# Two small reorderings in an attention and SwiGLU kernel: key sums scaled group by group, and the value copies of the first two batches dealt out anew between VectorE and ScalarE

## The chip, the cores and the metric

The kernel runs on one core of a Trainium2 chip. A core has TensorE (matrix products into eight PSUM banks), VectorE and ScalarE (which read PSUM and write SBUF), GpSimd ([...]it also issues most loads here) and SyncE (issues stores and transposing loads). The engines run side by side and wait for one another by semaphores; each works through its own instructions in order. The metric is the time of one execution on the device in microseconds; lower is better. Before the change it was 236.28 us, the median of four runs (235.95 to 236.55).

## The reference

For 8 batches of 8 heads, with 576 positions, head size 64 and 32 memory slots, attention goes over slots that are softmax-weighted sums of keys and values; its output, 4608 rows of 512, goes through a SwiGLU block with inner width 1536.

```python
a = exp(phi - max(phi)); a = a / (sum(a over slots) + 1e-9)
k_m = einsum('bhsm,bhsd->bhmd', a, k)
v_m = einsum('bhsm,bhsd->bhmd', a, v)
attn = softmax(q @ k_m.T / sqrt(64))
x = (attn @ v_m) as rows of 512
out = (silu(x @ w_gate) * (x @ w_val)) @ w_out
```

## The kernel before, in words

The kernel never forms `attn @ v_m`. It multiplies the memory values `v_m` of a batch into the gate and value weights first (a projection round, `u_round`, L454), which gives small matrices `U` for each batch, chunk of 512 inner columns and group of four heads; the attention weights `A` are then multiplied straight into `U`. Groups are called g = 0 and 1 throughout, and each has its own PSUM bank in a round.

The order of the work is written out by hand: Python calls emit instructions one after another, each engine's queue holds its instructions in that order, and there is no automatic reordering. PSUM banks come from a first-in, first-out list `free` of eight names: `bank` (L75) takes the first, `done` (L81) puts one back at the end. A matmul into a bank waits until the last instruction that read the bank's earlier tile has finished.

Loads of the first stage are issued by GpSimd in one sequence (L880 to L908): keys, queries and values of the first batches, then the weights, those of the first chunk in two halves (L897 to L899), those of the second and third chunks (L900 to L902), and the output weights.

**Batches 0 and 1** are prepared together. After their attention weights are there, the rounds of chunk 0 are split into halves of 256 columns and into gate (`which` 0) and value (`which` 1) parts, `u_half` (L829). Each such round makes 8 matmuls `p_u` into two banks, one per group, and copies each bank into `U` with the denominator as a scale (L488 on ScalarE for the letter "a", L492 on VectorE for "v"; the letters of `evac` go to the banks in order, group 0 first). The sequence is L945 to L957: gate round of batch 0 ("av"), of batch 1 ("vv"), four gates of batch 0 (`gv_gate`, L518: two matmuls `p_g`, a silu on ScalarE at L526), then the value rounds of batch 0 and 1, two gates of batch 1, then three value products (`flush_mul(3)`: two matmuls `p_v` each, and a product `t_h` on VectorE at L532), then the second half of chunk 0 for both batches, and so on. A `p_v` of batch 0 needs the value part of `U` of both groups of batch 0.

**Batches 2 to 7** are each taken through in one stage. Their memory keys and values come from `kv_sum` (L222): 72 matmuls add into two banks `p_kv0` and `p_kv1`, one per group, the keys in columns 0 to 63 and the values in columns 64 to 127; the denominators go into a corner of `p_kv0`. `kv_norm` (L268) then makes four scaled copies on VectorE (`scaled_copy`, L265): keys of group 0 (written twice side by side, 128 elements), keys of group 1, values of group 0 (64 elements), values of group 1. After it `run_sums` (L295) gives both banks back, and `kv_T` transposes the result: on TensorE up to batch 3, by a transposing transfer on SyncE after that. For batches 3 and 5 the denominators are made ahead of the sums and the copies precede the rest of the round; for batches 4, 6 and 7 another round stands between (`behind`). Beside all this run the gates and products of the batch before, whose slots take the banks as they come free, and the output products (L720).

Of the kernel before, what the change touches and what calls it, by code (L numbers as in the profile page):

```python
# [14 lines left out]
def kernel(  # L15
# [28 lines left out]
    NG = 2  # L44
# [30 lines left out]
    def bank(shape, dtype, name):  # L75
        tag = free.pop(0)
        t = ps.tile(shape, dtype, tag=tag, name=name)
        held[id(t)] = tag, t
        return t

    def done(*tiles):  # L81

        for t in tiles:
            free.append(held.pop(id(t))[0])
# [137 lines left out]
    def kv_sum(b, p, parts):  # L222


        w0, w1 = parts[0], parts[-1] + 1
        n = (w1 - w0) * D
        for j in range(JK):
            for i in range(NP):
                for g in range(NG):
                    nc.tensor.matmul(  # L230
                        p[g][32 * i:32 * i + 32, 0:n],
                        lhsT=phi_of(b, g, j, i),
                        rhs=kvs[b][64 * g:64 * g + 64, w0:w1, i, j * D:(j + 1) * D],
                        start=(j == 0),
                        stop=(j == JK - 1),
                        tile_position=(64 * g, 32 * i),
                    )

    def kv_denominators(b, p):

        if b in masked:
            for g in range(NG):
                for j in range(JK):
                    nc.tensor.matmul(
                        p[:, g:g + 1],
                        lhsT=masked[b][:, j, g].rearrange("p i m -> p (i m)"),
                        rhs=ones1,
                        start=(j == 0),
                        stop=(j == JK - 1),
                    )  # L250
            return
        if b in esums:
            hl = esums.pop(b)
            terms = [hl[:, t] for t in range(2)]
        else:
            terms = [ephis[b][:, j].rearrange("p i m -> p (i m)") for j in range(JK)]
        for n, x in enumerate(terms):
            nc.tensor.matmul(p, lhsT=x, rhs=ones2, start=(n == 0), stop=(n == len(terms) - 1))

    def kv_reciprocal(b, p):  # L260
        r = att.tile([128, NG], FP32, tag="rS", name="t_rS")
        nc.vector.reciprocal(out=r, in_=p)
        rSs[b] = r

    def scaled_copy(out, p, r):  # L265
        nc.vector.tensor_scalar(out=out, in0=p, scalar1=r, scalar2=None, op0=ALU.mult)  # L266

    def kv_norm(b, p):  # L268

        t = att.tile([128, 3, 128], BF16, tag="bkv", name="t_bkv")  # L270
        for g in range(NG):
            x = p[g][:, 0:D].rearrange("p (a d) -> p a d", a=1).to_broadcast([128, 2, D])
            scaled_copy(t[:, g].rearrange("p (a d) -> p a d", a=2), x, rSs[b][:, g:g + 1])
        for g in range(NG):
            scaled_copy(t[:, 2, D * g:D * g + D], p[g][:, D:2 * D], rSs[b][:, g:g + 1])
        bkvs[b] = t

    def kv_T(b):


        kTs[b] = att.tile([128, 3, 128], BF16, tag="kT", name="t_kT")
        t = bkvs.pop(b)
        if b > 3:
            nc.sync.dma_start_transpose(out=kTs[b], in_=t.rearrange("p n x -> p (n x)"))
            return
        p = bank([128, 3, 128], BF16, "p_T")
        for n in (2, 0, 1):
            nc.tensor.transpose(p[:, n], t[:, n], ident)
        nc.vector.tensor_copy(out=kTs[b], in_=p)
        done(p)  # L290

    def kv_items(b, beside=None):


        def run_sums():  # L295
            o = 2 * D
            p = [bank([128, CH], FP32, f"p_kv{g}") for g in range(NG)]
            behind = b in esums
            if not behind:
                kv_denominators(b, p[0][:, o:o + NG])  # L300
            kv_sum(b, p, (0, 1))
            if behind:
                beside()
                kv_denominators(b, p[0][:, o:o + NG])
            kv_reciprocal(b, p[0][:, o:o + NG])
            kv_norm(b, p)
            done(*p)
            if beside and not behind:
                beside()

        return [run_sums, lambda: kv_T(b)]
# [142 lines left out]
    def u_round(b, parts, evac):  # L454


        banks = []
        for which, c, halves in parts:
            w0, w1, h0, h1 = which[0], which[-1] + 1, halves[0], halves[-1] + 1
            n = (h1 - h0) * HC  # L460
            p = [bank([128, CH], FP32, f"p_u{g}") for g in range(NG)]
            for w in which:
                o = (w - w0) * n
                for i in range(NP):
                    for g in range(NG):
                        nc.tensor.matmul(  # L466
                            p[g][32 * i:32 * i + 32, o:o + n],
                            lhsT=kTs[b][64 * g:64 * g + 64, 2, 32 * i:32 * i + 32],
                            rhs=w_part(w, c, i, g, halves),
                            start=True,  # L470
                            stop=True,
                            tile_position=(64 * g, 32 * i),
                        )
            for g in range(NG):
                if (b, c, g) not in Us:
                    u_buffer(b, c, f"U{c}")
                if len(which) == 1:
                    dst = Us[b, c, g][:, h0:h1, w0]
                else:
                    dst = Us[b, c, g][:, h0]  # L480
                src = p[g][:, 0:(w1 - w0) * n].rearrange("p (a f) -> p a f", f=HC)
                banks.append((dst, src, p[g], rSs[b][:, g:g + 1] if b in scaled else None))
        for (t, p, home, r), e in zip(banks, evac):
            if e == "a":
                if r is None:
                    nc.scalar.copy(out=t, in_=p)  # L486
                else:
                    nc.scalar.activation(out=t, in_=p, func=AF.Copy, scale=r)  # L488
            elif r is None:
                nc.vector.tensor_copy(out=t, in_=p)  # L490
            else:
                nc.vector.tensor_scalar(out=t, in0=p, scalar1=r, scalar2=None, op0=ALU.mult)  # L492
            done(home)
# [24 lines left out]
    def gv_gate(b, s):  # L518

        jf, r = s // 2, s % 2  # L520
        c, o = jf // 4, jf % 4
        if o == 0 and r == 0:
            hts[b, c] = hpool.tile([128, 4, S], BF16, tag=f"h{c}", name="t_h")
        gate = gv_half(b, s, 0)
        sg = work.tile([128, HALF], BF16, tag="sg", bufs=8, name="t_sg")
        nc.scalar.activation(out=sg, in_=gate[:, 0:HALF], func=AF.Silu)  # L526
        done(gate)
        dst = hts[b, c][:, o, r * HALF:(r + 1) * HALF]

        def mul():  # L530
            val = gv_half(b, s, 1)
            nc.vector.tensor_tensor(out=dst, in0=sg, in1=val[:, 0:HALF], op=ALU.mult)  # L532
            done(val)
            if o == 3 and r == 1:
                chunk_done(b, c)

        pend.append(mul)
# [291 lines left out]
    def u_half(b, which, c, half, evac):  # L829

        return lambda: u_round(b, ((which, c, (half,)),), evac)
# [8 lines left out]
    def run(items):  # L840
        for x in items:
            x()
# [13 lines left out]
    def gv_slots(b):  # L856
        return [lambda s=s: gv_slot(b, s) for s in range(2 * NJF)]
# [90 lines left out]
    run([u_half(1, (0,), 0, 0, "vv")])  # L948
    for s in range(4):
        gv_gate(0, s)  # L950
    run([u_half(0, (1,), 0, 0, "va"), u_half(1, (1,), 0, 0, "va")])
    for s in range(2):
        gv_gate(1, s)
    flush_mul(3)
# [33 lines left out]
    for b in range(2, B):  # L988
# [59 lines left out]
        g = gv_slots(b)  # L1048
# [61 lines left out]
```

## Time and profile before

| | |
|---|---|
| median of four runs | 236.28 us (235.95 to 236.55) |
| the profiled execution | 236.13 us |
| its span, first to last instruction | 234.2 us |
| granted TensorE clock, mean | 0.995 |
| value matmuls `p_v`, 128x288 (L509) | 384 of 286 ns |
| silu of a gate (L526) | 192 of 424 ns |
| product `t_h` on VectorE (L532) | 192 of 451 ns |
| table load on ScalarE ahead of the silus (L946) | 1.28 us |
| scaled copies of the key sums (L266) | 24, of 273 to 352 ns |

Lengths of matmuls are from start to a modelled end, and they overlap: two of 128x288 that follow one another start 0.12 us apart. Instructions on VectorE and ScalarE overlap a little at their ends, too. A line of the timeline merges instructions of one kind that follow one another: its first number is the start, the second the time from there to the end of the last, `xN` their number. PE is TensorE's matmuls, PEld its weight loads, DVE VectorE, ACT ScalarE, POOL GpSimd. In a line of waits stand the engine and line that waited, who released it, the total in us, how many times, and the longest.

### The profile page before, as it was taken

How to read it: one execution, taken by the hardware profiler on the slowest of the kernel's cores; microseconds unless marked ns; L12 is line 12 of the kernel's file. 1: busy time of each engine (PE TensorE's matmuls, PEld its weight loads, DVE VectorE, ACT ScalarE, POOL GpSimd, SP SyncE). 2: the span in 40 equal slices, each digit the busy share in tenths (PEclk: the TensorE clock that was granted, in tenths of full speed). 3: DMA queues.
4: the chain of work that ended last, by engine and by line, in shares of the span. 5: the costliest groups of instructions: out<-in, count | busy, mean ns of one | idle time of the engine just before them, and what ended most of it. 6: DMA issues, size and time to landing. Idle time of an engine off the chain costs nothing.

```text
span 234.2 us, 7201 instructions
## 1 busy us (share of the span) xinstructions
PE 224.1 (96%) x2825; PEld 169.8 (73%) x2825; DVE 183.2 (78%) x421; ACT 173.7 (74%) x369; POOL 140.6 (60%) x190
## 2 busy tenths in 40 slices
PE   7987899999999999999999999999999999999992
PEld 2554466778887776878788787887788778878881
DVE  4155789999966698989797767999799879977732
ACT  2768788988447889968896658968898789677220
POOL 8422536998199059765966689464845494039390
PEclk9999999999999999999999999999999999999997
DMA  6999999999995992999099946995022702201224
GB/s 213 210 212 207 197 206 207 236 232 263 207 238 133 257 254 46 231 217 163 29 260 212 200 122 119 254 218 93 10 82 95 121 0 94 90 34 58 63 76 134
DMA packets 36610, 36.84 MB, mean 157 GB/s; under 512 B 14560, under 2 KB 30944, under 8 KB 36576
## 3 DMA queue, kind: packets, MB, share of 16 engines
q0 software_dynamic: 16272, 22.42, 51.5%
q1 hardware_dynamic: 19536, 13.18, 22.2%
q10 hardware_dynamic: 768, 0.79, 1.1%
q8 instruction: 22, 0.36, 0.6%
q14 instruction: 12, 0.10, 0.1%
HBM read 42.47 MB, written 9.44 MB: 222 GB/s over the span
## 4 chain that ended last, share of the span: by engine, by line
PE 86%; DMA 7%; ACT 2%; POOL 1%; DVE 1%; issue 1%; POOLq 0%
PE p_v L509 20%; PE p_os L720 20%; PE p_g L509 20%; PE p_oc L720 10%; DMA t_kv<-in_v_dram 7%; PE p_oa L720 5%; PE p_u L466 5%; PE p_kv L230 2%; PE p_g L390 1%; POOL t_kv L99 1%; DVE t_bkv L266 1%; PE p_mT L319 1%; PE p_warm L867 1%; ACT t_sg L526 1%; ACT L946 1%
## 5 line engine op out<-in xcount | busy, mean ns | idle before, releaser
L532 DVE TENSOR_TENSOR t_h<-t_sg,p_v 128x288 bf16<-128x288 bf16 x192 | 81.8, 451 | 17.9 <-PE p_v L509 6.9
L509 PEld LDWEIGHTS <-t_U 128*128 128x128 bf16 x768 | 73.6, 98 | 23.8 <-issue 3.8
L526 ACT ACTIVATE t_sg<-p_g 128x288 bf16<-128x288 f32 x192 | 74.0, 424 | 17.9 <-PE p_g L509 11.5
L509 PE MATMUL p_v<-t_A,t_U 128*128 128x288 bf16 x384 | 77.3, 286 | 0.4 <-ACT t_U L488 0.4
L509 PE MATMUL p_g<-t_A,t_U 128*128 128x288 bf16 x384 | 77.1, 286 | 0.6 <-ACT t_U L488 0.4
L720 PEld LDWEIGHTS <-t_S 128*128 128x128 bf16 x384 | 37.5, 98 | 4.5 <-issue 0.2
L597 POOL TENSOR_TENSOR t_S<-t_h 128x512 bf16<-128x512 bf16 x17 | 19.6, 1155 | 32.8 <-DVE t_h L532 32.7
L720 PEld LDWEIGHTS <-t_h 128*128 128x128 bf16 x288 | 27.1, 98 | 8.6 <-issue 5.0
L486 ACT CAST t_U<-p_u 128x512 bf16<-128x512 f32 x53 | 28.0, 607 | 6.6 <-PE p_u L466 6.6
L720 PE MATMUL p_os<-t_T,t_S 128*128 128x256 bf16 x192 | 23.7, 273 | 0.0
L554 POOL TENSOR_TENSOR t_S<-t_S,t_h 128x512 bf16<-128x512 bf16 x17 | 19.6, 1154 | 1.3
L554 POOL TENSOR_TENSOR t_S<-t_h,t_S 128x512 bf16<-128x512 bf16 x16 | 18.4, 1152 | 0.0
L554 POOL TENSOR_TENSOR t_S<-t_h 128x512 bf16<-128x512 bf16 x16 | 18.4, 1151 | 0.0
L466 PE MATMUL p_u<-W,t_kT 64*32 64x512 bf16 (+1 forms) x416 | 15.7, 364 | 0.3 <-DVE t_kT L333 0.3
L867 PE MATMUL p_warm<-bones 128*128 128x512 bf16 x44 | 13.3, 443 | 1.7 <-DVE bones L889 1.7
L720 PE MATMUL p_os<-t_T,t_h 128*128 128x256 bf16 x96 | 14.8, 273 | 0.0
L490 DVE CAST t_U<-p_u 128x512 bf16<-128x512 f32 x19 | 12.4, 683 | 1.9 <-PE p_u L466 1.9
L446 DVE TENSOR_TENSOR t_A<-t_E,t_lz 128x576 bf16<-128x576 bf16 x16 | 11.4, 739 | 0.7 <-ACT t_lz L422 0.7
L720 PE MATMUL p_oc<-t_T,t_S 128*128 128x256 bf16 x96 | 11.9, 273 | 0.0
L720 PE MATMUL p_oa<-WO,t_h 128*128 128x256 bf16 x96 | 11.8, 273 | 0.0
L720 PE MATMUL p_oc<-WO,t_S 128*128 128x256 bf16 x96 | 11.8, 272 | 0.1
L720 PE MATMUL p_os<-WO,t_h 128*128 128x256 bf16 x96 | 11.8, 272 | 0.0
(106 smaller groups left out, 308.5 us busy)
## 6 DMA issues: line engine op xcount, KB each, us to landing
out_dram<-t_o SPq DMA_DIRECT2D x15, 512.0 KB, 3.7
t_kv<-in_k_dram POOLq DMA_DIRECT2D x8, 576.0 KB, 10.3
t_q<-in_q_dram POOLq DMA_DIRECT2D x8, 576.0 KB, 8.7
t_kv<-in_v_dram POOLq DMA_DIRECT2D x8, 576.0 KB, 14.9
t_phi<-in_phi_dram POOLq DMA_DIRECT2D x6, 576.0 KB, 8.2
WO<-in_moe_w_out_dram POOLq DMA_DIRECT2D x3, 512.0 KB, 19.5
W<-in_moe_w_gate_dram POOLq DMA_DIRECT2D x2, 512.0 KB, 16.3
W<-in_moe_w_val_dram POOLq DMA_DIRECT2D x2, 512.0 KB, 16.2
```

What stands on the lines that cost most here:

```text
L230: nc.tensor.matmul(p[g][32 * i:32 * i + 32, 0:n], lhsT=phi_of(b, g, j, i), rhs=kvs[b][64 * g:64 * g + 64, w0:w1, i, j * D:(j + 1) * D], st ...
L446: nc.vector.tensor_tensor(out=a, in0=es.pop((b, g)), in1=lzs.pop((b, g)), op=ALU.mult)
L466: nc.tensor.matmul(p[g][32 * i:32 * i + 32, o:o + n], lhsT=kTs[b][64 * g:64 * g + 64, 2, 32 * i:32 * i + 32], rhs=w_part(w, c, i, g, halve ...
L486: nc.scalar.copy(out=t, in_=p)
L490: nc.vector.tensor_copy(out=t, in_=p)
L509: nc.tensor.matmul(p[:, 0:HALF], lhsT=Us[b, c, g][:, o // 2, which, 128 * (o % 2):128 * (o % 2 + 1)], rhs=atts[b, g][:, r], start=(g == 0) ...
L526: nc.scalar.activation(out=sg, in_=gate[:, 0:HALF], func=AF.Silu)
L532: nc.vector.tensor_tensor(out=dst, in0=sg, in1=val[:, 0:HALF], op=ALU.mult)
L554: eng.tensor_tensor(out=out, in0=x, in1=y, op=ALU.subtract)
L597: eng.tensor_tensor(out=t[:, 0], in0=A21, in1=A22, op=ALU.add)
L720: nc.tensor.matmul(mine[home][:, u], lhsT=lhs(c, m, u), rhs=rhs(c, m), start=fresh and u == 0, stop=(k == 5), skip_group_check=u == 1 or n ...
L867: nc.tensor.matmul(p[:, 0:128 * a], lhsT=bones, rhs=x.to_broadcast([128, a, 128]) if a > 1 else bones, start=True, stop=True,)
```

## The change

Two edits. In `kv_norm` the two copies of a group now follow one another (keys and values of group 0, then keys and values of group 1), and each group's bank is given back right after its copies, in place of both after the four. In the first stage the letters of the value rounds change: batch 0's copies both go to VectorE and batch 1's both to ScalarE, where each batch had one on either.

```diff
@@ kv_norm
         for g in range(NG):
             x = p[g][:, 0:D].rearrange("p (a d) -> p a d", a=1).to_broadcast([128, 2, D])
             scaled_copy(t[:, g].rearrange("p (a d) -> p a d", a=2), x, rSs[b][:, g:g + 1])
-        for g in range(NG):
             scaled_copy(t[:, 2, D * g:D * g + D], p[g][:, D:2 * D], rSs[b][:, g:g + 1])
+            done(p[g])
         bkvs[b] = t
@@ run_sums
             kv_reciprocal(b, p[0][:, o:o + NG])
             kv_norm(b, p)
-            done(*p)
             if beside and not behind:
                 beside()
@@ first stage
     for s in range(4):
         gv_gate(0, s)
-    run([u_half(0, (1,), 0, 0, "va"), u_half(1, (1,), 0, 0, "va")])
+    run([u_half(0, (1,), 0, 0, "vv"), u_half(1, (1,), 0, 0, "aa")])
     for s in range(2):
         gv_gate(1, s)
     flush_mul(3)
```

The banks come free in the same order as before, so every tile keeps its bank. On VectorE the second and third of the four scaled copies change places, in each of the six batches, and one copy of the first stage is that of another tile; on ScalarE one copy is that of another tile. TensorE's, GpSimd's and SyncE's instructions keep their order; on TensorE three instructions of the first stage wait for something else.

## The prediction

> **What bounds the kernel now.** I read the page's busy rows first, then the waits of TensorE and its weight loads, then the timeline of the two places that the change touches.
>
> ```profile
> PE 224.1 (96%) x2825; PEld 169.8 (73%) x2825; DVE 183.2 (78%) x421; ACT 173.7 (74%) x369; POOL 140.6 (60%) x190
> ```
>
> TensorE's instructions fill the span, and the chain that ended last is 86% TensorE. After the last warm-up stall, at 21.1 us, that chain leaves TensorE for only a few tenths at a time, so a hold of TensorE moves the end, and a microsecond of VectorE or ScalarE that holds nobody moves nothing. The waits of the matmuls (first fence) and of the weight loads (second) say which holds there are:
>
> ```profile
> PE p_v L509 <- ACT t_U L488: 0.4, 1, 0.4
> ```
>
> ```profile
> PEld L509 <- ACT t_U L488: 1.3, 2, 0.7
> PEld L509 <- DVE t_bkv L266: 0.8, 2, 0.4
> ```
>
> One hold of the value matmuls `p_v` by ScalarE's copy of a `t_U`, and two of 0.4 us by `t_bkv`. (The other hold in the 1.3 is at 26.5 us, in front of the first gate; the change leaves it.) The first of them, on the timeline of 23.5 to 36 us; columns are start, length from first start to last end, engine, line, operation, and in brackets the idle time before:
>
> ```profile
> 27.10 1.76 DVE L492 TENSOR_SCALAR t_U<-p_u,t_rS 128x256 bf16<-128x256 f32 x4
> 27.78 1.32 ACT L526 ACTIVATE t_sg<-p_g 128x288 bf16<-128x288 f32 x4
> 28.85 0.28 PE L509 MATMUL p_v<-t_A,t_U 128*128 128x288 bf16 x1
> 28.96 0.86 ACT L488 ACTIVATE t_U<-p_u,t_rS 128x256 bf16<-128x256 f32 x2
> 29.51 0.79 PE L509 MATMUL p_v<-t_A,t_U 128*128 128x288 bf16 x5 [0.38 <-ACT t_U L488]
> 29.67 0.75 ACT L526 ACTIVATE t_sg<-p_g 128x288 bf16<-128x288 f32 x2
> 29.92 1.18 DVE L532 TENSOR_TENSOR t_h<-t_sg,p_v 128x288 bf16<-128x288 bf16 x3 [1.06 <-ACT t_U L488]
> 30.23 0.63 PE L466 MATMUL p_u<-W,t_kT 64*32 64x256 bf16 x32
> 30.74 1.26 ACT L488 ACTIVATE t_U<-p_u,t_rS 128x512 bf16<-128x512 f32 x2 [0.32 <-PE p_u L466]
> 31.02 1.40 DVE L492 TENSOR_SCALAR t_U<-p_u,t_rS 128x512 bf16<-128x512 f32 x2
> ```
>
> VectorE's four copies are the gate pair of batch 1, then group 0 of the value round of batch 0, then group 0 of that of batch 1; starts 27.10, 27.49, 27.98, 28.38, end 28.86. ScalarE, late because of the table load at 26.49 (1.28 us), first does four silus and only then group 1 of batch 0 and group 1 of batch 1. So the first `p_v` gets its first matmul at 28.85 and its second, which needs group 1 of batch 0, at 29.51. Meanwhile VectorE has nothing to do for 1.06 us: it had copied batch 1's half, which nobody wants yet. The second place, on the timeline of 80.5 to 87 us (132 us looks the same):
>
> ```profile
> 82.12 0.99 DVE L266 TENSOR_SCALAR t_bkv<-p_kv,t_rS 128x128 bf16<-128x128 f32 x4
> 82.98 0.36 PEld L509 LDWEIGHTS <-t_U 128*128 128x128 bf16 x4 [0.37 <-DVE t_bkv L266]
> 83.24 0.41 PE L509 MATMUL p_v<-t_A,t_U 128*128 128x288 bf16 x2
> ```
>
> VectorE's four scaled copies start at 82.12, 82.39, 82.65 and 82.84. The gate at 82.98 takes the bank of `p_kv0`, given back by the third of them; the value matmuls at 83.24 take that of `p_kv1`, given back by the fourth at 82.12 + 0.99 = 83.11.
>
> **Part 1, the value rounds.** No instruction is added or removed: one 128x256 copy changes from ScalarE to VectorE (rows: 484 ns median there, 499 ns the shortest on ScalarE) and one comes back. No bank is handed out in another order, and TensorE's program differs only in what three instructions wait for.
> - VectorE now does group 1 of batch 0 in the slot of batch 1's group 0: 28.38 to 28.86. The bank rows show 0.05 to 0.08 us from an end to TensorE's restart (29.43 to 29.51 here, 82.93 to 82.98 there), so the second matmul may start at about 28.93, while unheld it would start at 28.97. The 0.54 us excess in 28.85 to 29.51 (0.66 less the 0.12 of one matmul) is gone.
> - What is late next: the second `p_v` takes the bank of the fourth silu, which ends at 29.10, so 29.17; TensorE is ready at 29.10. Behind this new wait stand the third `p_v` and the projection round; VectorE's products wait for them. Three `p_v` then end at 29.17 + 2 x 0.245 = 29.66 instead of 30.12, and the next projection round starts at about 29.77 instead of 30.23: gain 0.46.
> - Its banks: VectorE's (28.86), ScalarE's two copies, which end at about 29.43 and 29.82 as before, and that of the first silu of batch 1 (29.67 + 0.41 = 30.08, usable 30.15). So the second half of the round starts at 30.15 instead of 30.51: gain 0.36. The next `p_v` takes the bank of the second silu, 30.42 + 0.07 = 30.49 instead of 30.79: gain 0.30. ScalarE has become the limit, and it can win no more than its own idle 0.32 in front of 30.74.
> - Then a little comes back. After the casts at 31.02 to 32.42 TensorE's pairs, 0.245 us apart elsewhere, are 0.28, 0.29 and 0.36 apart three times up to 33.20, 0.20 us over, for banks that VectorE returns late. VectorE starts its three products at about 29.36 instead of 29.92 and its casts some 0.55 us earlier, against 0.30 for TensorE, so most of these holds go. Gain at the end of the stage between 0.30 and 0.50; I take 0.45, near the upper end, since the largest hold (33.20) waits on a product that VectorE then does half a microsecond sooner.
> - Of batch 1, both groups are now ScalarE's: group 0 is ready at 29.43 instead of 28.86. Its first reader is a product of TensorE at about 30.7, so 1.2 us of other work covers that. As a bank it is wanted at 29.77, with 0.27 to spare; without the cover it would cost what it is late.
> - Behind: the next round needs the value weights' second chunk. Its load was issued at 17.67 and took 16.9, so landed at 34.6; TensorE reads it at 35.01 + 0.28 = 35.29 now and at about 34.84 then. At the loads before, TensorE started 0.05 to 0.07 us after the landing, so there is 0.15 us left: this caps the gain at about 0.6.
>
> **Part 2, the key sums.** The same 24 copies, in another order. A 128-wide copy is followed by the next after 0.27 us, a 64-wide one after 0.19. So the copies start at 82.12, 82.39, 82.58 and 82.84, `p_kv0` comes back with the second (about 82.67 instead of 82.93) and `p_kv1` with the fourth, as before at 83.11. The gate starts at about 82.72, 0.26 us sooner, and then the value matmuls wait for 83.16: won are 83.24 - 83.16 = 0.08, less some 0.015 for starting anew. The Trainium skill's page "PSUM — Partial Sum Buffer" (section "PSUM bank collisions raise a hardware error") bears on this: readers and writers are kept apart by bank, not by address. If only the first returned bank counted, the two places would give 2 x 0.26 = 0.52; with the second bank held to the fourth copy, as rule and row have it, 2 x 0.065 = 0.13. Below nothing it could go if a second stop of TensorE exposed a whole weight load (98 ns in the row): 2 x (0.08 - 0.10) = -0.04. I take 0.13, because the restart at 82.98 reached its next pair after 0.26 us against 0.245 in the unheld row. In the other four batches the four copies move past nothing: at 60.9 the next user is the transposes, which read all four results, and at 106, 159 and 183 us the banks are taken again only later, with no wait in the rows. VectorE's products behind the four copies start as before. No DMA is moved, and the queues of SP and GpSimd are unchanged.
>
> A rule against any gain is in "Perfetto Trace Analysis", section "Identifying the Most-Contended Engine": work on the engine of highest occupancy. Here that is TensorE, of whose work nothing is removed; by that rule alone the sum is 0 and the time 236.13. The rows show the holds by name (0.38 + 0.37 + 0.40), on the engine that sets the end; so I count these, of which the above gives back half.
>
> **Sum.** The profiled execution took 236.13 us (span 234.2 and 1.9 around it). 0.45 + 0.13 = 0.58 off: 235.55. That execution lies 0.15 below the median of 236.28; for the median, 235.70. After 34 us nothing that I find takes it back: TensorE has no wait over 0.4 us, and the last sums on GpSimd start behind VectorE's sums, which start behind TensorE.
>
> **Rivals.**
> - The gain is lost on the way (no change). ScalarE is busy without a break from 26.0 to 30.42; if the holds up to 33.20 are ScalarE's and not VectorE's, and the second stops of part 2 cost a weight load each, 0.30 - 0.04 = 0.26 remains: 236.02; a landing at 34.8 would take 0.1 more. For it: every bank that TensorE wants from 29.1 to 30.5 is ScalarE's. Against: VectorE, not ScalarE, is the later one at 33.20.
> - Slower: the weight load sets the pace at 35 us. TensorE arrives there sooner, and if the second value chunk lands at L, the round starts at L + 0.07 instead of 35.29. From L = 35.22 the gain of part 1 is gone, and with part 2's 0.13 it is slower by over 0.47 us from L = 35.8; L = 36 gives 236.28 + 0.78 - 0.13 = 236.93. For it: the weight loads took 15.5 to 19.8 us, a spread of 4.3. Against: nothing in the change touches their issue, all before 25 us, and the runs before lie within 0.6 us.
> - More: both banks of the key sums count in full, 0.50 + 0.52: 235.26. Against it stands the fourth copy at 83.11.
>
> **Numbers.** About 0.2%, or 0.47 us, is what a measurement of this kernel can tell from no change. Forecast 0.58 off (taken between 0.34 and 0.65): chance 0.65, of which some 0.08 falls short of 0.47. No change 0.19, slower 0.11, more 0.05. So faster 0.62, within 0.27, slower 0.11. The range from 235.2 to 236.4 takes in the first, second and fourth case and leaves out the slower one and some scatter.
>
> **What would show it.** Right: the wait of `p_v` for ScalarE's `t_U` is gone, the three `p_v` stand together by 29.7, the projection round near 29.8 and the next near 34.55; at 82 us the gate starts near 82.7 instead of 82.98, and the value matmuls follow after a second short stop, under 0.1 us sooner than now. Wrong: a wait for a weight load at 34.6, a new hold by ScalarE at 30 to 33, or the next rounds (35.0, 39.6) standing where they stand now.

## The result, and the profile after

The changed kernel takes 235.81 us (median of 28 runs, 235.47 to 236.50), against 236.35 for the kernel before in 46 runs: a ratio of 0.9979, 95% interval 0.9973 to 0.9984, or 0.50 us faster (0.38 to 0.64). The forecast was 0.58 us less than 236.28, or 235.70. The profiled execution took 235.82 us with a span of 233.9.

TensorE is still what fills the span, and the hold of `p_v` by ScalarE's `t_U` is gone: the waits of the matmuls have no line of `p_v` any more (first fence: the page; second: waits of the weight loads):

```profile
PE 223.4 (95%) x2825; PEld 169.6 (73%) x2825; DVE 183.3 (78%) x421; ACT 173.7 (74%) x369; POOL 140.6 (60%) x190
```

```profile
PEld L508 <- ACT t_U L487: 0.7, 1, 0.7
PEld L508 <- DVE t_bkv L266: 0.7, 2, 0.3
```

Of ScalarE's `t_U` only the wait ahead of the first gate is left. The two stops by `t_bkv` are still there, now 0.3 instead of 0.4 at the most. (All line numbers after L307 are one lower than before.) The value rounds, on the timeline of 26.9 to 36 us:

```profile
27.40 1.76 DVE L491 TENSOR_SCALAR t_U<-p_u,t_rS 128x256 bf16<-128x256 f32 x4
29.15 0.95 PE L508 MATMUL p_v<-t_A,t_U 128*128 128x288 bf16 x6
29.26 0.86 ACT L487 ACTIVATE t_U<-p_u,t_rS 128x256 bf16<-128x256 f32 x2
29.67 1.18 DVE L531 TENSOR_TENSOR t_h<-t_sg,p_v 128x288 bf16<-128x288 bf16 x3 [0.51 <-PE p_v L508]
30.04 0.85 PE L465 MATMUL p_u<-W,t_kT 64*32 64x256 bf16 x32
30.48 0.14 PEld L465 LDWEIGHTS <-t_kT 64*32 64x32 bf16 x14 [0.21 <-issue]
30.55 1.32 ACT L487 ACTIVATE t_U<-p_u,t_rS 128x512 bf16<-128x512 f32 x2
32.79 0.41 PE L508 MATMUL p_g<-t_A,t_U 128*128 128x288 bf16 x2
33.03 0.41 PE L508 MATMUL p_v<-t_A,t_U 128*128 128x288 bf16 x2
34.84 0.63 PE L465 MATMUL p_u<-W,t_kT 64*32 64x512 bf16 x16
```

The same stretch before, the lines that are compared with these (timeline of 23.5 to 36 us):

```profile
26.53 1.15 PE L509 MATMUL p_g<-t_A,t_U 128*128 128x288 bf16 x8 [0.36 <-ACT t_U L488]
32.84 0.41 PE L509 MATMUL p_g<-t_A,t_U 128*128 128x288 bf16 x2
33.20 0.41 PE L509 MATMUL p_v<-t_A,t_U 128*128 128x288 bf16 x2
35.01 0.62 PE L466 MATMUL p_u<-W,t_kT 64*32 64x512 bf16 x16
```

The three `p_v` stand together in one row of six matmuls. The projection round behind them begins at 30.04 and stops once, at 30.48, at its second half. After it ScalarE goes on without a break (0.32 us idle before), so ScalarE is now the one that is waited for. From 32.8 the pairs are 0.245 us apart; the 0.29 and 0.36 of before, up to 33.20, are gone. The key sums of batch 3, timeline of 80 to 84.5 us:

```profile
81.95 0.99 DVE L266 TENSOR_SCALAR t_bkv<-p_kv,t_rS 128x128 bf16<-128x128 f32 x4
82.58 0.41 PE L508 MATMUL p_g<-t_A,t_U 128*128 128x288 bf16 x2
83.00 0.11 PEld L508 LDWEIGHTS <-t_U 128*128 128x128 bf16 x2 [0.32 <-DVE t_bkv L266]
83.00 0.42 PE L508 MATMUL p_v<-t_A,t_U 128*128 128x288 bf16 x2
```

The gate no longer waits, it follows its forerunner at the usual distance; the value matmuls behind it wait until the fourth copy ends at 81.95 + 0.99 = 82.94. The stop has moved one step down and lost little.

The span is only 0.3 us shorter than that of before, although both stages won what was expected. The rest lies ahead of the changed instructions, on the timeline of 24 to 27 us:

```profile
25.94 0.41 PE L465 MATMUL p_u<-W,t_kT 64*32 64x256 bf16 x16 [0.47 <-DMA W<-in_moe_w_gate_dram]
26.83 1.15 PE L508 MATMUL p_g<-t_A,t_U 128*128 128x288 bf16 x8 [0.48 <-ACT t_U L487]
```

The first gate stands at 26.83, at 26.53 before: the projection round ahead of it waited for the first weights, which took 19.8 us here and 19.5 there. The change touches nothing ahead of this, and over eleven kernels with the same loads the first gate lies anywhere between 26.52 and 26.99. So the stages are compared by their own lengths. The table gives, from one profiled execution each, the us from the first gate to the projection round of chunk 1 (A), from there to the sums of batch 3 (B), from these to the next twelve `p_os` (C), and the same for batch 5 (D); the last column is the ratio of the timed runs with its interval.

| kernel | first gate | A | B | C | D | ratio to before |
|---|---|---|---|---|---|---|
| before | 26.53 | 8.48 | 46.13 | 11.29 | 14.89 | |
| the change | 26.83 | 8.01 | 46.13 | 11.24 | 14.84 | 0.9979 (0.9973 to 0.9984) |
| value rounds alone | 26.94 | 8.01 | 46.14 | 11.29 | 15.00 | 0.9980 (0.9973 to 0.9988) |
| key sums alone | 26.70 | 8.49 | 46.14 | 11.23 | 14.83 | 0.9998 (0.9989 to 1.0006) |
| value rounds the other way | 26.99 | 8.85 | 46.13 | 11.29 | 14.89 | 1.0021 (1.0011 to 1.0030) |
| table load early, as before otherwise | 26.81 | 7.79 | 46.13 | 11.29 | 14.95 | 0.9975 (0.9965 to 0.9984) |
| table load early and the change | 26.53 | 7.91 | 46.17 | 11.24 | 15.02 | 0.9981 (0.9974 to 0.9987) |
| table load early and key sums | 26.52 | 7.89 | 46.13 | 11.24 | 14.84 | 0.9971 (0.9962 to 0.9981) |
| change, group 1 scaled on ScalarE | 26.91 | 8.01 | 46.13 | 11.47 | 15.23 | 0.9999 (0.9991 to 1.0008) |
| the same, casts two and two | 26.75 | 8.02 | 46.13 | 11.16 | 14.80 | 0.9971 (0.9962 to 0.9979) |
| the last with early load, old deal | 26.97 | 7.79 | 46.13 | 11.17 | 14.75 | 0.9954 (0.9940 to 0.9967) |

In the change A is 0.47 shorter and C and D 0.05 each, 0.57 together; less the 0.30 by which this execution began later, that is the 0.27 to 0.3 between the two spans. B does not move: nothing is taken back.

A and C repeat from profile to profile: C is 11.29 in all four kernels with the old order of the scaled copies and 11.23 or 11.24 in the four with the new order alone. D scatters: 14.89 to 15.00 with the old order, 14.83 to 15.02 with the new. At batch 5 itself the value matmuls start 2.17 us after the sums with the old order and 2.10 or 2.11 with the new, in every one of these profiles; the scatter lies behind that, and its cause stays open. So the gain at batch 5 shows at its place, as 0.06 or 0.07, while the length D can hide it.

### The profile page after: what moved, and what is told of

Read it like the earlier page. It is cut to its first block, busy times and chain, and to the rows that moved or that the text cites. A ratio compares the mean times of both kernels' runs of the same rounds, so it can differ in the third digit from the quotient of the medians.

```text
span 233.9 us, 7201 instructions
## 1 busy us (share of the span) xinstructions
PE 223.4 (95%) x2825; PEld 169.6 (73%) x2825; DVE 183.3 (78%) x421; ACT 173.7 (74%) x369; POOL 140.6 (60%) x190
## 4 chain that ended last, share of the span: by engine, by line
PE 86%; DMA 8%; POOL 2%; ACT 1%; issue 0%; DVE 0%; POOLq 0%
PE p_v L508 21%; PE p_g L508 21%; PE p_os L719 20%; PE p_oc L719 10%; DMA W<-in_moe_w_gate_dram 8%; PE p_u L465 5%; PE p_oa L719 5%; PE p_kv L230 2%; PE p_g L389 1%; POOL t_kv L99 1%; POOL t_kv L103 1%; PE p_q L376 0%; POOL t_q L108 0%; ACT t_qT L330 0%; PE p_kv L258 0%
## 5 line engine op out<-in xcount | busy, mean ns | idle before, releaser
L866 PE MATMUL p_warm<-bones 128*128 128x512 bf16 x44 | 12.6, 423 | 1.7 <-DVE bones L888 1.7
```

What stands on the lines that cost most here:

```text
L866: nc.tensor.matmul(p[:, 0:128 * a], lhsT=bones, rhs=x.to_broadcast([128, a, 128]) if a > 1 else bones, start=True, stop=True,)
```

## The experiments

**The value rounds alone and the key sums alone.** Each edit of the change without the other.

```diff
-    run([u_half(0, (1,), 0, 0, "va"), u_half(1, (1,), 0, 0, "va")])
+    run([u_half(0, (1,), 0, 0, "vv"), u_half(1, (1,), 0, 0, "aa")])
```

> Only the letters of the two value rounds are changed (batch 0 to VectorE, batch 1 to ScalarE); the key sums stay as before. Theory (one hold of 0.54 us by ScalarE goes, 0.1 to 0.2 of it comes back as waits for ScalarE's banks, the holds up to 33 us go): 0.45 us faster than before, ratio 0.9981. From the first gate to the next projection round (8.48 us before) it takes about 8.0. Rival (the key sums give the larger share): 0.1 to 0.2 us faster, and 8.3 or more in that stretch.

A is 8.01, 0.47 shorter, and the ratio 0.9980 is 0.47 us: the value rounds give nearly all. D is 0.11 longer than before, with no instruction of that stage changed: this is the scatter named above.

> Only the order of the four scaled copies is changed; the value rounds stay as before. Theory (the hold moves from the gate to the value matmuls, which wait for the fourth copy): 0.06 us faster at each of two places, 0.12 in all, ratio 0.9995. Rival 1 (each group's bank counts in full): 0.5 faster, 0.9978. Rival 2 (a second stop costs a weight load each): 0 to 0.05 slower.

C and D are 0.06 shorter each, 0.12 in all, as the theory said. The timed ratio leaves open whether this is a gain (0.26 us faster to 0.14 slower), but excludes the 0.5 of the first rival. It does not exclude the second (0 to 0.05 slower); against that stand only the lengths C and D. The parts add up: 0.9980 and 0.9998 make 0.9978.

**The value rounds the other way.** Batch 0 to ScalarE, batch 1 to VectorE.

```diff
-    run([u_half(0, (1,), 0, 0, "va"), u_half(1, (1,), 0, 0, "va")])
+    run([u_half(0, (1,), 0, 0, "aa"), u_half(1, (1,), 0, 0, "vv")])
```

> The value rounds dealt out the other way round: batch 0 to ScalarE, batch 1 to VectorE; key sums as before. Theory (ScalarE is late by its table load and four silus, whoever it copies for): both groups of batch 0 come from ScalarE, the second at 29.8 instead of 29.4, so the first value product is complete 0.39 us later than before; 0.2 to 0.45 us slower, ratio 1.0015. Rival (what helps is only that one engine does both copies of a batch): 0.3 or more faster, as in the change.

Slower, 1.0021: A is 0.37 longer. Its timeline of 28.5 to 31.5 us:

```profile
29.98 1.15 PE L509 MATMUL p_v<-t_A,t_U 128*128 128x288 bf16 x6 [0.56 <-ACT t_U L488]
30.34 0.48 PEld L509 LDWEIGHTS <-t_U 128*128 128x128 bf16 x5 [0.27 <-ACT t_U L488]
```

TensorE waits once for each of ScalarE's two copies. So what helps is not that one engine does both copies of a batch, but that batch 0's copies do not come from the late ScalarE.

**The table load early.** In the kernel before, ScalarE is idle ahead of the first gate round's copy, and the table load comes behind that copy:

```profile
26.00 0.47 ACT L488 ACTIVATE t_U<-p_u,t_rS 128x256 bf16<-128x256 f32 x1 [1.13 <-PE p_u L466]
26.49 1.28 ACT L946 ACT_TABLE_LOAD   x1
```

In this kernel the load goes into the idle stretch instead, and the letters of that gate round are swapped with it; all else is as before.

```diff
-    run([u_half(0, (0,), 0, 0, "av")])
     nc.scalar.preload_act_table_set("silu_and_others")
+    run([u_half(0, (0,), 0, 0, "va")])
```

> The kernel before, with ScalarE's table load one step ahead of the first gate round's copies, where ScalarE is idle for 1.13 us, and the letters of that round swapped (group 0 to VectorE), so that the copy that comes after the load is the one that is needed second. Value rounds and key sums as before. Theory (the table load makes ScalarE late, and that alone makes the hold): ScalarE begins its silus about 0.8 us sooner, copies group 1 of batch 0 by 28.8, the hold of the first value product is gone without a new deal; 0.4 to 0.6 us faster, ratio 0.998. Rival (ScalarE is late for another reason, such as the gates themselves): within 0.1 of before.

0.9975, and A 0.69 shorter: in that stage more than the new deal gives, though the intervals of the timed ratios overlap. On its timeline of 26 to 31 us:

```profile
27.26 1.32 ACT L526 ACTIVATE t_sg<-p_g 128x288 bf16<-128x288 f32 x4 [0.49 <-PE p_g L509]
28.44 0.86 ACT L488 ACTIVATE t_U<-p_u,t_rS 128x256 bf16<-128x256 f32 x2
28.99 0.90 PE L509 MATMUL p_v<-t_A,t_U 128*128 128x288 bf16 x6
29.82 0.63 PE L466 MATMUL p_u<-W,t_kT 64*32 64x256 bf16 x32
```

With the old deal, ScalarE's copies begin at 28.44 instead of 28.96, though the first gate is 0.28 later, and TensorE runs through: no stop in the `p_v`, none in the round (0.63 us; 0.85 in the change). ScalarE's lateness was the table load, and it made the hold. (Swapping the letters of the gate round alone was not run.)

> The changed kernel, and also the table load one step earlier and the letters of the first gate round swapped. Theory (in the changed kernel ScalarE's banks are the next limit, worth 0.1 to 0.2 us at 30 us): 0.1 to 0.2 us faster than the change, 0.6 to 0.7 faster than before, ratio 0.9972; the second half of the projection round follows its first without a stop. Rival (the next weight chunk, or VectorE's returns up to 33 us, is the limit already): same as the change, 0.9979.

The same early load on top of the change: 0.9981, no faster than the change, so the rival is right. Its timeline of 26 to 33 us:

```profile
28.72 1.02 PE L508 MATMUL p_v<-t_A,t_U 128*128 128x288 bf16 x6
28.94 0.48 PEld L508 LDWEIGHTS <-t_U 128*128 128x128 bf16 x5 [0.25 <-DVE t_U L491]
32.27 0.40 PE L508 MATMUL p_g<-t_A,t_U 128*128 128x288 bf16 x2
32.64 0.40 PE L508 MATMUL p_v<-t_A,t_U 128*128 128x288 bf16 x2
```

The projection round runs without its stop, but the late pairs are back: 0.29 us up to 32.27 and 0.37 up to 32.64. From the start of this round to that of chunk 1 it is 4.78 us, as in the kernel before and with the early load alone; in the change, with the stop and without the late pairs, it is 4.80. So ScalarE's stop was worth nothing in the end: what it costs is saved at the late pairs, and the reverse. That these wait for banks returned by VectorE, as the rival has it, is argued from the order of the work; no recorded wait names it.

A is 7.91: 0.10 less than in the change, and 0.12 more than with the early load alone. The 0.12 has a recorded wait. The new deal makes the second matmul of the first `p_v` wait at 28.94 for VectorE's fourth copy, which ends at about 28.89, and the six `p_v` take 1.02 us where they took 0.90. Once ScalarE is on time, the new deal costs about 0.1 us in this stage, by one trace each; the timed ratios cannot tell 0.9981 from 0.9975. The 0.04 us by which its B is longer may be the weight chunk, which landed at about 34.6; no wait is recorded there.

> The new order of the scaled copies, and in the first stage not the new deal but the earlier table load with the letters of the first gate round swapped. Theory (the two gains do not meet: 0.69 in the first stage as read from the trace of the kernel with the earlier load alone, and 0.1 from the scaled copies): 0.7 to 0.8 us faster than before, ratio 0.9968, and faster than the change. Rival (the loads of the first stage limit both): as the change, 0.9979.

Early load and key sums: 0.9971, near the expected 0.9968 and faster than the key sums alone; from the early load alone (0.9975) and from the change the intervals do not part it. A is 7.89, not 7.79: here the first weights came soonest, ScalarE's copy starts only at 26.31, when the table load of 25.02 ends, and a weight load at 26.84 waits 0.22 us for it. ScalarE's value copies then begin 1.84 us after the first gate (1.63 with the early load alone), and the six `p_v` take 0.98 us instead of 0.90. So, by this one trace, the load can come too late even in its new place.

**What is left at the key sums.** In the changed kernel, group 1's two scaled copies of batches 3 and 5 go to ScalarE.

```diff
+            beside = g == 1 and b in (3, 5)
+            both = scaled_copy_a if beside else scaled_copy
-            scaled_copy(t[:, 2, D * g:D * g + D], p[g][:, D:2 * D], rSs[b][:, g:g + 1])
+            both(t[:, 2, D * g:D * g + D], p[g][:, D:2 * D], rSs[b][:, g:g + 1])
```

(The key copies likewise; `scaled_copy_a` is `nc.scalar.activation` with Copy and the scale.)

> The changed kernel, with both scaled copies of group 1 on ScalarE in batches 3 and 5 (the two where TensorE stops), ahead of its four casts there. Theory (what is left of the stop is the fourth copy on VectorE): the bank of group 1 comes back some 0.3 us sooner, the value matmuls follow the gate with no stop; about 0.25 us faster at each place less what ScalarE's casts, 0.5 us later, give back: 0.2 to 0.5 us faster than the change, 0.7 to 1.0 faster than before, ratio 0.9965. Rival (the casts that come later hold TensorE as long): no faster than the change, 0.9979 or above.

No faster than before: 0.9999. The timeline of 81 to 85 us shows both halves:

```profile
82.09 0.57 ACT L269 ACTIVATE t_bkv<-p_kv,t_rS 128x128 bf16<-128x128 f32 x2 [0.95 <-PE p_u L470]
82.56 1.56 ACT L490 CAST t_U<-p_u 128x512 bf16<-128x512 f32 x3
82.91 0.41 PE L513 MATMUL p_v<-t_A,t_U 128*128 128x288 bf16 x2
83.68 0.41 PE L513 MATMUL p_g<-t_A,t_U 128*128 128x288 bf16 x2 [0.16 <-ACT t_U L490]
```

The value matmuls start without a wait, so the fourth copy on VectorE was indeed what was left. But ScalarE's three casts end at 84.12, and the gate at 83.68 waits for one of their banks. C and D are 0.23 and 0.39 longer than in the change.

Then the four casts of the round beside these copies are dealt two and two in those batches:

> As the kernel with group 1's scaled copies on ScalarE in batches 3 and 5, but the four casts of the round beside them are dealt two to VectorE and two to ScalarE in those batches, where ScalarE had three. Theory (what that kernel lost is ScalarE's casts coming 0.5 us later): ScalarE ends its casts at the time of the change again, the stops at 83 and 132 us are gone, 0.2 to 0.4 us faster than the change, ratio 0.9965. Rival (VectorE's products, 0.3 to 0.6 us later by the second cast, hold the banks instead): no faster than the change, 0.9979 or above.

```diff
-                (kv_items(b + 1, lambda: (u_item(b, 2, "aava")(), run(take(2)))), KV, KV + 4),
+                (kv_items(b + 1, lambda: (u_item(b, 2, "avav" if b in (2, 4) else "aava")(), run(take(2)))), KV, KV + 4),
```

0.9971 (the interval overlaps that of the change). On its timeline of 80.8 to 84 us:

```profile
82.34 1.28 DVE L494 CAST t_U<-p_u 128x512 bf16<-128x512 f32 x2
82.41 1.07 ACT L490 CAST t_U<-p_u 128x512 bf16<-128x512 f32 x2
83.21 0.41 PE L513 MATMUL p_g<-t_A,t_U 128*128 128x288 bf16 x2
83.53 0.41 PE L513 MATMUL p_v<-t_A,t_U 128*128 128x288 bf16 x2
```

Both engines end their casts within 0.15 us of each other and the recorded stops are gone; 83.21 to 83.53 is still 0.08 over the usual distance. In C and D it gains 0.08 and 0.04 on the change, 0.12 of the 0.2 to 0.4 expected: the theory's direction holds, its size was too large.

**What helped, together.** The early load, the old deal, the new order of the scaled copies, group 1 on ScalarE and the casts two and two.

> What helped, together: the earlier table load in place of the new deal of the value copies, the new order of the scaled copies, and in batches 3 and 5 group 1's scaled copies on ScalarE with the casts dealt two and two. Theory (the gains lie at different places and add up): from the first gate to the next projection round 7.8 to 7.9 us (8.48 before, 8.01 in the change), from the sums of batch 3 to the output products 11.16 (11.29, 11.24); 0.8 to 0.95 us faster than before, ratio 0.9963. Rival (some of it is taken back where batches meet): as the better of the parts, 0.9971.

235.43 us against 236.45 in the same session, ratio 0.9954 (0.9940 to 0.9967; 5 runs of it), the fastest kernel of this study. A, C and D are 0.69, 0.12 and 0.14 shorter, 0.95 together, or 0.9960.

## Why the prediction was right, step by step

- **What bounds it.** Right: from the sum of a row of the table (first gate, A to D) to the start of the last copy on VectorE it is 122.40 to 122.42 us in all eleven profiles, so every stage difference shows up at the end. The zero that the prediction took from the Trainium skill's "Perfetto Trace Analysis", section "Identifying the Most-Contended Engine", reads too much into it: the section says which engine to optimize first, not that only removed work counts, and it judges TensorE's headroom by FLOP rate and weight loads (73% busy here) instead of busy matmuls (96%). The holds of TensorE gave 0.57 us.
- **The first value product.** Right. Reckoned from the first gate, the round was to start at 29.77 - 26.53 = 3.24 us and started at 3.21; its second half at 3.62 and started at 3.65 (30.48 - 26.83); the round of chunk 1 at 8.02 and started at 8.01. That ScalarE makes this stop is shown by the early load on top of the change, which takes it out of the round. Nothing was won by that, as the late pairs up to 33 us then come back.
- **Some comes back up to 33 us.** Right, by the step forecast: VectorE's products start 2.84 us after the first gate (3.39 before), 0.55 sooner, where TensorE is 0.27 sooner at its next `p_v`. The pairs are even, and 0.47 was won where I took 0.45.
- **The cap by the value weights' chunk.** Not reached: in three kernels the round of chunk 1 started at 34.60 or sooner without a recorded wait for it.
- **The key sums.** Right in kind: from the start of the sums, the gate was to come after 1.65 us (1.68 measured) and the value matmuls after 2.09 (2.10). 0.10 in the change and 0.12 alone, 0.13 predicted. The Trainium skill's "PSUM — Partial Sum Buffer" (section "PSUM bank collisions raise a hardware error") has PSUM guarded by bank, not by address, and the rows agree: the gate at 82.58 takes the first bank while VectorE reads the second until 82.94, and the value matmuls wait for the last reader of the second.
- **Nothing takes it back later.** Right: B (but for the 0.04 named above) and the stretch from the end of D to the start of the last copy on VectorE (84.24 or 84.25 us everywhere) stay the same, and only D scatters in some kernels.
- **The sum.** 0.58 predicted, 0.57 in the stages, 0.50 timed (0.38 to 0.64). What the sum did not hold is the front: the profiled execution before had one of the earliest first gates of all, 26.53, so the forecast for a single execution, 235.55, missed by 0.27: in the one that was then profiled the weights landed later and the first gate stood 0.30 later. Of the 0.11 between the forecast and the measured median, 0.07 is the median of the kernel before, 236.35 in 46 runs where four gave 236.28. I took the two executions' fronts for equal, which no row said.

I did not see that the better cure stood in a row I quoted: the table load at 26.49, with ScalarE idle for 1.13 us ahead of the one copy in front of it. I treated its place as given and worked around it, as the change does.

## What to carry to other kernels

When an engine is late at a hand-over, look at its queue from the idle stretch before: moving a fixed cost (here a table load) into that stretch won 0.69 us of that stage where dealing its work to the neighbour won 0.47, and with the first done the second wins nothing more. A stop that disappears is worth its length only if no later hold comes back: look at the length of the whole stage. Where two buffers are wanted one after the other, giving back the first sooner wins only up to the moment when the second comes back. And a copy moved to an idle engine also moves whatever stands behind it there: deal those out anew in the same step.

## What I had not expected of the hardware

The landing of the first loads sets the start of the first gate. In ten of the eleven profiles the first weights landed 19.5 to 19.9 us after their issue at 6.0 us, and the projection round started some 0.1 to 0.2 us later; in the one with early load and key sums they took 19.3, and the round stopped for `t_kT`, made from the values. The first gate lay between 26.52 and 26.99 us in eleven profiles of kernels with the same loads, nearly as much as the whole change is worth. Differences under half a microsecond are better read as lengths between landmarks behind the last load than as spans.
